# Sparse attention with a feed-forward block in split fp32: who issues the fetches of the weights, and where in a step they are converted

## The chip, the cores and the metric

The kernel runs on one core of a Trainium2 chip. The metric is the device time of one execution in microseconds (us). The engines are TensorE (PE, with its weight loads PEld), VectorE (DVE), ScalarE (ACT), GpSimd (POOL) and SyncE (SP); each works through its own instructions in the order in which they are written. SP computes nothing: before the change it issues most of the transfers.

## The reference

```python
# attention, per batch and head: B, H, S, D = 4, 8, 768, 64, blocks of 32
scores = scale * (q @ k^T)              # masked to: own block and its two neighbours, block 0 and the last,
                                        # 3 sampled blocks per block; rows of block 0 and the last see all
attn = exp(scores - max); attn /= sum + 1e-9
x = (attn @ v), as 3072 tokens x 512
# feed-forward: w_in 512 x 2048, w_out 2048 x 512, both float64
h = x @ w_in
out = (h * sigmoid(1.702 * h)) @ w_out  # float32
```

## The kernel before

**Steps of attention.** The 3072 tokens are 48 units of 64 tokens; a unit takes two steps (four for the units of the first and last blocks, which see all keys), 104 steps in all. A step t of the sparse kind does 16 small products of q and k (L252), takes the bias and the row's minimum on VectorE (L271, nm), exponentials on ScalarE (L284, ex), four transposes on PE (L299), their copy on ScalarE (L312, pt), and 32 products with V (L330). These are staggered: `tick` writes the scores of step t, the values of step t-2, then the transposes and the pt copy of step t-1. A finished unit is normalised (L347 to L350), turned (L360) and split into a high and a low fp32r part (L365 xhi, L366 xlo).

**Chunks of the feed-forward.** Eight units make a chunk of 512 tokens. For each of 6 chunks and each of 16 slices f of the hidden dimension there is one step m: `up` (12 matmuls, L447 to L449), `gate` (L455 on ScalarE, L456 on VectorE), its split (L461 ghi, L469 glo), and for the slice before, `down` (12 matmuls, L484 to L490). Beside each step m runs about one step of attention for the next chunk. The attention of the first chunk, 16 steps and two more, stands ahead of it all: the lead-in, with `early` true, in which score and transpose banks alternate. Then come the 16 steps of the first chunk's feed-forward, and so on.

**The weights.** They come as float64 and are turned into two fp32r parts, high and low. `weights` is a generator: each `next` writes one piece of work, up to a `yield`. It works through 32 conversions k, alternating slices of w_in and w_out: `todo` is (0, in), (1, in), (0, out), (2, in), (1, out) and so on. Conversion k has five pieces:

- ScalarE takes the absolute value of the high words of conversion k+1 (`first(k + 1)`, L393, a<-raw); VectorE limits it for k (L413)
- VectorE masks and shifts (L415)
- VectorE makes the low part of conversion k-1 (`last(k - 1)`, L398); for w_out both parts are then stored to a scratch tensor ws (L400); conversion k+2's words are fetched (`fetch(k + 2)`, L386, raw, 512 KB, one of three buffers)
- VectorE puts in the sign (L422)
- VectorE puts in the low words' bits (L425); ScalarE rounds to the high part (L428)

Before, the fetch and the store are on SP's queue. w_in's parts stay on the chip (`win`, 16 tiles); w_out's parts go through a ring of four tiles (`wout`), are stored, and come back from ws for the chunks after the first (L494). A w_out slice f is only converted when `down` of slice f-4 has been written, so a piece can do nothing for a while. `run` sets the pace: 3 pieces in a step of the lead-in, written between the scores and the transposes (`run(n0)`, ahead of `after`), and in the first chunk 4 ahead of the transposes and 4 at the end of each step m (`run(n1)`).

**K and V.** Each pair of batches has an entry per unit: K is 256 KB of q (L184) and 12 blocks of 128 KB (L186 to L196; the six sampled ones at addresses read from the table, L196), V is one direct part (vmid, L210 and L212) and two indirect gathers by POOL (vown, L214). Two buffers each: entry n+2 is loaded when entry n's last step is done, four steps ahead of its use. `loads` is called at the end of each step, and writes all K entries that are due, then all V entries. At the very start two of each are due: K0, K1, V0, V1. In the lead-in three of the six sampled K blocks are issued by POOL.

**Landing counters.** The transfers of SP and ScalarE share eight landing counters, taken in turn; a transfer is only issued when the one that last used its counter has landed.

Of the kernel before, what the change touches and what calls it, by code (L numbers as in the profile page):

```python
# [9 lines left out]
F32 = mybir.dt.float32  # L10
# [17 lines left out]
NF = DF // P  # L28
# [6 lines left out]
RING = 2  # L35
WRING = 4
# [7 lines left out]
class Kernel:  # L44
# [172 lines left out]

    def loads(self, t):

        while self.knext < len(self.kent) and (self.knext < RING or self.kent[self.knext - RING]["last"] <= t):  # L220
            self.load_k(self.kent[self.knext])
            self.knext += 1
        while self.vnext < len(self.vent) and (self.vnext < RING or self.vent[self.vnext - RING]["last"] <= t - 2):
            self.load_v(self.vent[self.vnext])
            self.vnext += 1

# [141 lines left out]
    def weights(self):  # L370

        nc = self.nc
        todo = []
        for f in range(NF + LAG):
            if f < NF:
                todo.append((f, 0))
            if f >= LAG:
                todo.append((f - LAG, 1))
        self.ready = set()
        tiles = {}  # L380

        def fetch(k):
            if k < len(todo):
                f, i = todo[k]
                raw = self.work.tile([P, 2 * DM], I32, name="raw", bufs=3)
                nc.sync.dma_start(out=raw, in_=self.w64[i][f])  # L386
                tiles[k] = {"raw": raw.rearrange("p (a b) -> p a b", b=2)}

        def first(k):

            if k < len(todo):
                a = tiles[k]["a"] = self.work.tile([P, DM], I32, name="a", bufs=3)
                nc.scalar.activation(out=a.bitcast(F32), in_=tiles[k]["raw"][:, :, 1].bitcast(F32), func=AF.Abs)  # L393

        def last(k):
            f, i = todo[k]
            t, w = tiles[k]["t"], tiles.pop(k)["a"].bitcast(F32)
            nc.vector.tensor_tensor(out=t[:, DM:2 * DM], in0=w, in1=t[:, 0:DM].bitcast(F32), op=ALU.subtract)  # L398
            if i == 1:
                nc.sync.dma_start(out=self.ws[f], in_=t.bitcast(F32))  # L400
            self.ready.add((f, i))

        for k in range(3):
            fetch(k)
        yield
        first(0)
        for k, (f, i) in enumerate(todo):
            while i == 1 and f - WRING > self.downs - 1:
                yield
            first(k + 1)  # L410
            raw, a = tiles[k]["raw"], tiles[k]["a"]
            low, high = raw[:, :, 0], raw[:, :, 1]
            nc.vector.tensor_scalar(out=a.bitcast(F32), in0=a.bitcast(F32), scalar1=FMIN, scalar2=None, op0=ALU.max)  # L413
            yield
            nc.vector.tensor_scalar(out=a, in0=a, scalar1=0x07FFFFFF, scalar2=3, op0=ALU.bitwise_and,  # L415
                                    op1=ALU.logical_shift_left)
            yield
            if k > 0:
                last(k - 1)
                fetch(k + 2)  # L420
                yield
            nc.vector.scalar_tensor_tensor(out=a, in0=high, scalar=-0x40000000, in1=a, op0=ALU.bitwise_and,  # L422
                                           op1=ALU.bitwise_or)
            yield
            nc.vector.scalar_tensor_tensor(out=a, in0=low, scalar=29, in1=a, op0=ALU.logical_shift_right,  # L425
                                           op1=ALU.bitwise_or)
            t = tiles[k]["t"] = self.win[f] if i == 0 else self.wout[f % WRING]
            nc.scalar.copy(out=t[:, 0:DM], in_=a.bitcast(F32))  # L428
            yield
        last(len(todo) - 1)  # L430

    def need(self, f, i):
        while (f, i) not in self.ready:
            next(self.conv, None)
# [88 lines left out]
    def tick(self, ts, m, n0, n1):  # L523
# [6 lines left out]
        for k in range(max(1, len(ts))):  # L530
            t = ts[k] if ts else None
            late = k == max(1, len(ts)) - 1
            un = None
            if t is not None:
                if have(t):
                    self.scores(t)
                if have(t - 2):
                    self.values(t - 2)
                    if self.steps[t - 2]["end"]:
                        un = self.steps[t - 2]["unit"]  # L540
            if late and moe:
                self.up(m)
            if un is not None:
                self.normalise(un)
            run(n0)
            after = []
            if t is not None:
                if have(t - 1):
                    after += self.transposes(t - 1)
                if un is not None:  # L550
                    after += self.turn(un)
            if late and moe:
                self.gate(m)
            for f in after:
                f()
            if t is not None:
                self.loads(t)
        if m is not None:
            if m >= LAG:
                self.down(m - LAG)  # L560
            if moe:
                self.gate_hi(m)
        run(n1)

    def run(self):
        self.g, self.downs = {}, 0
        self.conv = self.weights()
        self.indices()
        self.loads(-1)
        t = 0  # L570
        while t < self.ends[0] + LEAD:
            if t == 2:
                next(self.conv)
            self.tick([t], None, 3 if t > 3 else 0, 0)
            t += 1
        self.early = False
        total = len(self.steps) + 2
        for m in range(NC * NF + LAG):
            c, f = divmod(m, NF)
            if c + 1 < NC:  # L580
                goal = self.ends[c] + LEAD + (self.ends[c + 1] - self.ends[c]) * (f + 1) // NF
            else:
                goal = total
            ts = list(range(t, min(goal, total)))
            t = max(t, min(goal, total))
            self.tick(ts, m, 4 if c == 0 else 0, 4 if c == 0 else 0)

# [49 lines left out]
```

## Time and profile before

| | |
|---|---|
| median of 3 runs | 865.1 us (864.77 to 866.31) |
| the profiled execution | 869.51 us, its span 867.9 us |
| granted TensorE clock, mean | 0.965 |
| busy: PE, PEld, DVE, ACT, POOL | 783.5, 576.8, 374.3, 339.8, 57.5 us |
| moved by DMA | 153.38 MB, mean 177 GB/s |

The page shows the span in 40 slices of 21.7 us, each digit a busy share in tenths. A wait is put down to whatever ended it: "PE bank L330 <- ACT pt L312: 23.5, 9, 8.6" is 23.5 us in which PE, ahead of an instruction of line 330, waited for ScalarE's pt, in 9 pieces, the longest 8.6 us. SPq is SP's queue of issues. In rows of the timeline the two numbers ahead are start and duration in us, and the bracket behind is idle time and what ended it. Steps can be counted in the timeline by the first products of each step (L252) in the lead-in, and by the gates (L455) in the chunks.

### The profile page before, as it was taken

The page shows a single profiled execution, that of the slowest core. Times are in us where ns is not written, and L with a number is a line of the kernel's source. Part 1 is how long each engine was busy: PE and PEld are TensorE (multiplying, and loading weights), DVE is VectorE, ACT ScalarE, POOL GpSimd, SP SyncE. Part 2 cuts the span into 40 slices and gives each one's busy share as a digit, 9 for nine tenths or more (in the row PEclk, how much of TensorE's full clock was granted, in tenths as well). Part 3 has the DMA queues.
Part 4 walks back from the last instruction along what each step waited for, and adds up shares of the span by engine and source line. Part 5 has one row for each costly group of instructions (what it writes and reads, how often), then busy time and mean ns, then how long its engine had stood idle before and what let it go on. Part 6 is the DMA issues. An engine that isn't in the chain of part 4 may idle for free.

```text
span 867.9 us, 19160 instructions
## 1 busy us (share of the span) xinstructions
PE 783.5 (90%) x7584; PEld 576.8 (66%) x7584; DVE 374.3 (43%) x1026; ACT 339.8 (39%) x853; POOL 57.5 (7%) x85
## 2 busy tenths in 40 slices
PE   2547788788799999999999999999999999999996
PEld 0324556566576766767777777777776666778885
DVE  2466767667653333334333343333343343332222
ACT  2445544455443334334433344333443433322221
POOL 4121100100000000010000000000000000000000
PEclk9986889998999999999999999999999999999999
DMA  8887766666666444486655547454657432233221
GB/s 238 291 252 247 249 199 205 213 203 184 216 205 209 174 158 137 140 266 176 214 160 167 182 150 237 146 180 147 205 160 249 164 112 87 85 117 102 97 98 49
DMA packets 64285, 153.38 MB, mean 177 GB/s; under 512 B 7922, under 2 KB 29683, under 8 KB 63683
## 3 DMA queue, kind: packets, MB, share of 16 engines
q1 hardware_dynamic: 56962, 126.64, 46.0%
q0 software_dynamic: 7232, 25.51, 9.2%
q8 instruction: 60, 0.98, 0.5%
q14 instruction: 31, 0.25, 0.1%
HBM read 137.44 MB, written 14.68 MB: 175 GB/s over the span
## 4 chain that ended last, share of the span: by engine, by line
PE 74%; DMA 9%; DVE 5%; SPq 4%; ACT 3%; issue 3%; POOL 1%; POOLq 0%; ACTq 0%; DVEq 0%
PE bank L447 11%; PE bank L484 9%; PE bank L485 9%; PE bank L449 9%; PE bank L448 9%; PE bank L490 8%; DMA raw<-in_moe_w_in_dram 5%; PE bank L330 5%; PE bank L252 5%; PE bank L299 4%; PE bank L263 3%; DMA raw<-in_moe_w_out_dram 2%; DMA vown<-in_v_dram,vidx 1%; PE bank L337 1%; DVE bank L271 1%
## 5 line engine op out<-in xcount | busy, mean ns | idle before, releaser
L456 DVE SCALAR_TENSOR_TENSOR g<-g,bank 128x512 f32<-128x512 f32 x96 | 66.1, 688 | 282.1 <-ACT g L455 282.1
L447 PE MATMUL bank<-xhi,win 128*128 128x512 f32 x384 | 162.5, 423 | 0.0
L484 PE MATMUL bank<-wout,ghi 128*128 128x512 f32 x384 | 159.1, 414 | 0.0
L448 PE MATMUL bank<-xlo,win 128*128 128x512 f32 x384 | 152.4, 397 | 0.0
L449 PE MATMUL bank<-xhi,win 128*128 128x512 f32 x384 | 152.4, 397 | 0.0
L485 PE MATMUL bank<-wout,ghi 128*128 128x512 f32 x384 | 152.0, 396 | 0.0
L284 ACT ACTIVATE ex<-bank,nm 128x256 f32<-128x256 f32 x176 | 81.7, 470 | 164.5 <-DVE nm L271 163.3
L455 ACT ACTIVATE g<-bank 128x512 f32<-128x512 f32 x96 | 57.3, 597 | 177.5 <-PE bank L449 177.4
L271 DVE CUSTOM_DVE_ANT_1 bank<-bank,bias 128x256 f32<-128x256 f32 x176 | 71.5, 448 | 84.1 <-PE bank L252 76.2
L490 PE MATMUL bank<-wout,glo 128*128 128x512 f32 x360 | 98.6, 395 | 0.0
L252 PE MATMUL bank<-kg,qt 64*32 64x256 f32 x1408 | 65.9, 422 | 30.6 <-ACT pt L312 17.7
L447 PEld LDWEIGHTS bank<-xhi,win 128*128 128x128 f32 x384 | 73.7, 192 | 20.6 <-issue 0.5
L449 PEld LDWEIGHTS bank<-xhi,win 128*128 128x128 f32 x384 | 73.6, 192 | 17.0
L448 PEld LDWEIGHTS bank<-xlo,win 128*128 128x128 f32 x384 | 74.2, 193 | 13.1
L330 PEld LDWEIGHTS bank<-vown,pt 128*32 128x32 f32 x1408 | 32.5, 116 | 75.1 <-issue 33.7
L469 DVE TENSOR_TENSOR glo<-g,ghi 128x512 fp32r<-128x512 f32 x96 | 66.4, 691 | 36.7 <-ACT ghi L461 36.3
L485 PEld LDWEIGHTS bank<-wout,ghi 128*128 128x128 f32 x384 | 73.0, 190 | 13.4
L484 PEld LDWEIGHTS bank<-wout,ghi 128*128 128x128 f32 x384 | 72.7, 189 | 13.6
L214 POOL DMA_INDIRECT vown<-in_v_dram,vidx x44 | 44.3, 1007 | 563.9 <-PE bank L330 446.6
L330 PE MATMUL bank<-vown,pt 128*32 128x64 f32 x1408 | 52.0, 237 | 32.8 <-ACT pt L312 24.4
L490 PEld LDWEIGHTS bank<-wout,glo 128*128 128x128 f32 x360 | 68.1, 189 | 16.2
L312 ACT COPY pt<-bank 128x512 f32<-128x512 f32 (+1 forms) x120 | 65.2, 556 | 14.7 <-PE bank L299 11.2
(69 smaller groups left out, 753.2 us busy)
## 6 DMA issues: line engine op xcount, KB each, us to landing
wout<-ws SPq DMA_DIRECT2D x80, 512.0 KB, 3.4
kg<-in_kb_dram SPq DMA_DIRECT2D x158, 128.0 KB, 3.1
raw<-in_moe_w_in_dram SPq DMA_DIRECT2D x16, 512.0 KB, 5.6
raw<-in_moe_w_out_dram SPq DMA_DIRECT2D x16, 512.0 KB, 5.7
ws<-wout SPq DMA_DIRECT2D x16, 512.0 KB, 4.1
kg<-in_kb_dram SPq DMA_DIRECT2D x26, 256.0 KB, 4.1
kg<-in_kT_dram SPq DMA_DIRECT2D x4, 1536.0 KB, 7.8
vown<-in_vd_dram SPq DMA_DIRECT2D x8, 768.0 KB, 5.5
```

What stands on the lines that cost most here:

```text
L252: nc.tensor.matmul(sps[h][BLK * c:BLK * (c + 1), 0:n].rearrange("p (g n s) -> p g n s", g=2, n=4), self.qt[r][rows, bi, UT * pair + BLK * ...
L271: nc.vector.tensor_tensor_reduce(out=at, in0=at, in1=bias, scale=-SCALE, scalar=3.0e38, op0=ALU.add, op1=ALU.min, accum_out=nm[:, c:c + 1])
L284: nc.scalar.activation(out=ex, in_=sms[c], func=AF.Exp, bias=least[c], scale=-1.0, accum_out=sums[c])
L330: nc.tensor.matmul(av[BLK * c:BLK * (c + 1), 2 * i + h], pt[:, 2 * h + k, BLK * c:BLK * (c + 1)], src[:, at:at + D], start=(k == 0), stop= ...
L447: nc.tensor.matmul(h, wih[:, k], hi[:, k], start=(k == 0), stop=False)
L448: nc.tensor.matmul(h, wih[:, k], lo[:, k], start=False, stop=False)
L449: nc.tensor.matmul(h, wil[:, k], hi[:, k], start=False, stop=(k == NCT - 1))
L456: nc.vector.scalar_tensor_tensor(out=g, in0=g, scalar=1.0, in1=self.h, op0=ALU.add, op1=ALU.mult)
L469: self.nc.vector.tensor_tensor(out=glo, in0=g, in1=ghi.bitcast(F32), op=ALU.subtract)
L484: nc.tensor.matmul(o[n], ghi[:, tk[n]], woh, start=(f == 0), stop=False)
L485: nc.tensor.matmul(o[n], ghi[:, tk[n]], wol, start=False, stop=False)
L490: nc.tensor.matmul(o[n], glo[:, tk[n]], woh, start=False, stop=False)
```

## The change

Four things change. The fetches of words (`fetch`) are issued by ScalarE instead of SP. The stores of w_out's parts are issued by ScalarE too, and written later: conversion k's store stands in conversion k+2, behind its fetch, as a function `save` of its own. `loads` takes K and V entries in turn, so the start has K0, V0, K1, V1. And in the lead-in the three pieces of conversion stand at the end of a step, behind the transposes, the pt copy and `loads`, instead of ahead of the transposes. What is left of the conversion after the 16 steps of the first chunk is written out ahead of the next step.

```diff
     def loads(self, t):
-        while self.knext < len(self.kent) and (self.knext < RING or self.kent[self.knext - RING]["last"] <= t):
-            self.load_k(self.kent[self.knext])
-            self.knext += 1
-        while self.vnext < len(self.vent) and (self.vnext < RING or self.vent[self.vnext - RING]["last"] <= t - 2):
-            self.load_v(self.vent[self.vnext])
-            self.vnext += 1
+        more = True
+        while more:
+            more = False
+            if self.knext < len(self.kent) and (self.knext < RING or self.kent[self.knext - RING]["last"] <= t):
+                self.load_k(self.kent[self.knext])
+                self.knext += 1
+                more = True
+            if self.vnext < len(self.vent) and (self.vnext < RING or self.vent[self.vnext - RING]["last"] <= t - 2):
+                self.load_v(self.vent[self.vnext])
+                self.vnext += 1
+                more = True
...
-                nc.sync.dma_start(out=raw, in_=self.w64[i][f])
+                nc.scalar.dma_start(out=raw, in_=self.w64[i][f])
...
             nc.vector.tensor_tensor(out=t[:, DM:2 * DM], in0=w, in1=t[:, 0:DM].bitcast(F32), op=ALU.subtract)
+            self.ready.add((f, i))
+
+        def save(k):
+            f, i = todo[k]
             if i == 1:
-                nc.sync.dma_start(out=self.ws[f], in_=t.bitcast(F32))
-            self.ready.add((f, i))
+                nc.scalar.dma_start(out=self.ws[f], in_=self.wout[f % WRING].bitcast(F32))
...
                 last(k - 1)
                 fetch(k + 2)
                 yield
+            if k > 1:
+                save(k - 2)
...
+        save(len(todo) - 2)
         last(len(todo) - 1)
+        yield
+        save(len(todo) - 1)
...
-            self.tick([t], None, 3 if t > 3 else 0, 0)
+            self.tick([t], None, 0, 3 if t > 3 else 0)
...
+            if m == NF:
+                for _ in self.conv:
+                    pass
```

The lines behind the edits move down, by 5 at L284 (now L289) and by 13 at L455 (now L468). POOL's queue at the start, before: kg_93 is K0's buffer, kg_94 K1's, vown_97 and vown_98 V0's and V1's (each sampled block is read from the table, then issued).

```order
L196 DMA kg_93<-in_kb_dram 128x256
L195 TENSOR_LOAD sbr
L195 ISA x2
L196 ISA
L196 DMA kg_94<-in_kb_dram 128x256
...
L196 DMA kg_94<-in_kb_dram 128x256
L214 DMA vown_97<-in_v_dram,vidx 128x1024 x2
L214 DMA vown_98<-in_v_dram,vidx 128x1024 x2
```

And after:

```order
L196 DMA kg_93<-in_kb_dram 128x256
L214 DMA vown_97<-in_v_dram,vidx 128x1024 x2
L195 TENSOR_LOAD sbr
L195 ISA x2
L196 ISA
L196 DMA kg_94<-in_kb_dram 128x256
...
L196 DMA kg_94<-in_kb_dram 128x256
L214 DMA vown_98<-in_v_dram,vidx 128x1024 x2
```

V0's two gathers now stand behind K0's last block, ahead of K1's three. ScalarE in the lead-in, before, two steps (ex is L284, pt L312):

```order
L284 ACTIVATE ex,rs<-bank_85,nm 128x256
L284 ACTIVATE ex,rs<-bank_86,nm 128x256
L393 ACTIVATE a<-raw 128x512
L312 COPY pt<-bank_92 128x512
L284 ACTIVATE ex,rs<-bank_89,nm 128x256
L284 ACTIVATE ex,rs<-bank_90,nm 128x256
L428 CAST win_104<-a 128x512
L393 ACTIVATE a<-raw 128x512
L312 COPY pt<-bank_88 128x512
```

And after, the same place (ex is L289, pt L317, a<-raw L398, the cast L438):

```order
L289 ACTIVATE ex,rs<-bank_85,nm 128x256
L289 ACTIVATE ex,rs<-bank_86,nm 128x256
L317 COPY pt<-bank_92 128x512
L398 ACTIVATE a<-raw 128x512
L391 DMA raw<-in_moe_w_in_dram 128x1024
L289 ACTIVATE ex,rs<-bank_89,nm 128x256
L289 ACTIVATE ex,rs<-bank_90,nm 128x256
L317 COPY pt<-bank_88 128x512
L370 CAST xhi_121<-bank_91 128x4x64
L438 CAST win_104<-a 128x512
L398 ACTIVATE a<-raw 128x512
```

The conversion's rows stand behind pt instead of ahead of it, and the fetch stands in this queue, one step ahead of the row that uses its words. ScalarE in the first chunk, before (g is the gate, ghi its high part):

```order
L393 ACTIVATE a<-raw 128x512
L284 ACTIVATE ex,rs<-bank_85,nm 128x256
L284 ACTIVATE ex,rs<-bank_86,nm 128x256
L428 CAST wout_117<-a 128x512
L393 ACTIVATE a<-raw 128x512
L455 ACTIVATE g<-bank_92 128x512
L312 COPY pt<-bank_85 128x512
L461 CAST ghi<-g 128x512
L428 CAST win_107<-a 128x512
```

And after:

```order
L398 ACTIVATE a<-raw 128x512
L391 DMA raw<-in_moe_w_out_dram 128x1024
L409 DMA ws_72<-wout_120 128x1024
L289 ACTIVATE ex,rs<-bank_85,nm 128x256
L289 ACTIVATE ex,rs<-bank_86,nm 128x256
L438 CAST wout_117<-a 128x512
L398 ACTIVATE a<-raw 128x512
L391 DMA raw<-in_moe_w_in_dram 128x1024
L468 ACTIVATE g<-bank_92 128x512
L317 COPY pt<-bank_85 128x512
L474 CAST ghi<-g 128x512
L438 CAST win_107<-a 128x512
```

Each fetch now stands behind the use of the words fetched before it, and a store stands right behind a fetch; the rest keeps its order.

## Prediction

> **What bounds the kernel now.** I began with the page's slices, to see which part of the span has time to win.
>
> ```profile
> PE   2547788788799999999999999999999999999996
> DMA  8887766666666444486655547454657432233221
> ```
>
> TensorE (PE) is saturated from about slice 12 (250 us) to the end; what can move lies before. There I took a table by stage (busy time of PE, PEld, DVE, ACT, POOL, then granted clock, DMA share, GB/s): the start, the rest of the lead-in (attention of the first chunk), the first chunk's feed-forward with the conversion of the weights, and a stretch behind it.
>
> ```profile
> 0.00:29.00 29.00, 7.58 (x88) 3.50 (x88) 6.12 (x34) 4.72 (x14) 10.28 (x33) 1.00 0.89 259
> 29.00:93.00 64.00, 39.36 (x805) 23.64 (x812) 41.12 (x133) 34.61 (x99) 15.13 (x20) 0.80 0.81 259
> 93.00:250.00 157.00, 133.66 (x1280) 97.37 (x1280) 105.37 (x252) 74.61 (x173) 9.64 (x9) 0.91 0.66 210
> 250.00:310.00 60.00, 57.32 (x653) 42.43 (x652) 23.69 (x72) 25.17 (x67) 1.87 (x2) 1.00 0.59 191
> ```
>
> PE is idle for 21, 25 and 23 us in the first three stages, and no engine is full there. So waits decide. Who waits in the lead-in (total, times, longest):
>
> ```profile
> PE bank L330 <- ACT pt L312: 23.5, 9, 8.6
> ACT a L393 <- DMA raw<-in_moe_w_in_dram: 7.3, 2, 6.3
> ```
>
> and in the first chunk:
>
> ```profile
> ACT a L393 <- DMA raw<-in_moe_w_in_dram: 24.2, 9, 5.2
> PE bank L252 <- ACT pt L312: 15.1, 8, 4.1
> ACT a L393 <- DMA raw<-in_moe_w_out_dram: 15.7, 4, 6.2
> PE bank L299 <- ACT ex L284: 7.3, 4, 4.0
> SPq L400 <- DVE wout L398: 72.8, 9, 11.3
> ```
>
> This is one chain: SP's queue stands still at a store (L400) until VectorE has made the second half of a weight, a fetch (L386) behind it goes out late, ScalarE stands at L393 until the words land, and PE stands at what ScalarE has queued behind (pt, ex). One place shows it, SP, ScalarE and PE in turn:
>
> ```profile
> 143.67 6.05 SPq L196 DMA_DIRECT2D kg<-in_kb_dram  x6
> 149.82 0.38 SPq L386 DMA_DIRECT2D raw<-in_moe_w_out_dram  x1
> 153.82 0.66 ACT L393 ACTIVATE a<-raw 128x512 f32<-128x512 f32 x1 [3.98 <-DMA raw<-in_moe_w_out_dram]
> 154.98 0.66 PE L299 MATMUL bank<-ident,ex 128*128 128x128 f32 x4 [4.01 <-ACT ex L284]
> ```
>
> Here it is six K loads that hold the fetch up, and the 4 us end on PE. The fetch itself took 4.0 us (149.82 to 153.82); over all, the median landings are
>
> ```profile
> raw<-in_moe_w_in_dram SPq DMA_DIRECT2D x16, 512.0 KB, 5.6
> raw<-in_moe_w_out_dram SPq DMA_DIRECT2D x16, 512.0 KB, 5.7
> ```
>
> **The change part by part.** The profiled execution took 869.5 us (span 867.9, 1.6 around it), 4.4 us over the median of 865.1; I sum differences on the profile and take them off the median.
>
> *K and V in turn.* Rows of POOL, ScalarE and PE at the start:
>
> ```profile
> 9.72 0.54 POOL L196 DMA_DIRECT2D kg<-in_kb_dram  x1 [0.64 <-issue]
> 13.21 1.01 POOL L214 DMA_INDIRECT vown<-in_v_dram,vidx  x1 [0.58 <-issue]
> 17.45 0.58 ACT L312 COPY pt<-bank 128x512 f32<-128x512 f32 x1
> 26.95 0.43 PE L330 MATMUL bank<-vown,pt 128*32 128x64 f32 x5 [2.75 <-DMA vown<-in_v_dram,vidx]
> ```
>
> PE could start its first values when pt is copied (18.0) and starts them in full at 26.95, when V has landed. The change puts V's two gathers ahead of the second K's three loads on POOL, at 9.72 instead of 13.21: 3.5 us at least. If V then lands before pt, 8.9 us. The second K must then land later, but is first needed two steps on. I take 5, nearer the lower end, since the DMA share there is 0.89 and the landing is mostly a backlog. **-5** (-8.9 to -3.5).
>
> *Lead-in: conversion behind the step, fetches on ScalarE.* From the first row to the second it runs 15 steps in 63.9 us; the other four rows serve the next part.
>
> ```profile
> 29.00 1.11 PE L252 MATMUL bank<-kg,qt 64*32 64x256 f32 x16
> 92.88 1.11 PE L252 MATMUL bank<-kg,qt 64*32 64x256 f32 x16
> 99.91 0.60 ACT L455 ACTIVATE g<-bank 128x512 f32<-128x512 f32 x1 [1.03 <-PE bank L449]
> 242.72 0.60 ACT L455 ACTIVATE g<-bank 128x512 f32<-128x512 f32 x1 [0.31 <-PE bank L449]
> 250.31 0.60 ACT L455 ACTIVATE g<-bank 128x512 f32<-128x512 f32 x1 [1.95 <-PE bank L449]
> 265.23 0.60 ACT L455 ACTIVATE g<-bank 128x512 f32<-128x512 f32 x1 [1.93 <-PE bank L449]
> ```
>
> Without its waits for words a step is (63.9 - 7.3)/15 = 3.8 us. pt now goes ahead of the conversion, so a late word no longer holds values; next late is the following step's ex, which PE needs a step later. On ScalarE a fetch stands one step ahead of its use, so each of 7 fetches waits for its landing less 3.8. Landing 4.0 (the row at 149.82): 1.4 us in all, against 7.3: -6. Landing 5.7: 13.3, +6. Transfers bound the gain: 259 GB/s over 64 us is 16.6 MB, which at the best slice's 291 GB/s takes 57 us:
>
> ```profile
> GB/s 238 291 252 247 249 199 205 213 203 184 216 205 209 174 158 137 140 266 176 214 160 167 182 150 237 146 180 147 205 160 249 164 112 87 85 117 102 97 98 49
> ```
>
> I take a landing of 4.7, above the one below, as the DMA share is 0.81 here and 0.66 there (6.3 us of waits, -1), and 2 us for the cover that the new place gives: **-3** (-7 to +6).
>
> *First chunk.* 15 steps in 142.8 us (99.91 to 242.72), 9.52 each; undisturbed they take 7.45 (250.31 to 265.23 is two). So 31 us can be won at most. What a conversion costs, by line:
>
> ```profile
> L393 ACT ACTIVATE a<-raw 128x512 f32<-128x512 f32 x32 | 21.2, 666 | 47.3 <-DMA raw<-in_moe_w_in_dram 31.4 <-DMA raw<-in_moe_w_out_dram 15.7
> L428 ACT CAST win<-a 128x512 fp32r<-128x512 f32 x16 | 9.9, 619 | 18.7 <-DVE a L425 18.7
> L425 DVE SCALAR_TENSOR_TENSOR a<-raw,a 128x512 int32<-128x512 int32 x32 | 22.1, 690 | 0.8
> L422 DVE SCALAR_TENSOR_TENSOR a<-raw,a 128x512 int32<-128x512 int32 x32 | 22.0, 686 | 0.0
> L398 DVE TENSOR_TENSOR wout<-a,wout 128x512 fp32r<-128x512 f32 x16 | 11.0, 687 | 1.2 <-ACT wout L428 1.2
> L415 DVE TENSOR_SCALAR a<-a 128x512 int32<-128x512 int32 x32 | 13.7, 429 | 0.9
> L413 DVE TENSOR_SCALAR a<-a 128x512 f32<-128x512 f32 x32 | 13.5, 421 | 4.9 <-ACT a L393 4.9
> ```
>
> A conversion has 5 pieces and a step runs 8, so 1.6 conversions per step, one per 4.65 us. A fetch stands 3 pieces ahead of the use of its words: 2.8 us. Two things change in opposite senses. Gone is all that held a fetch in SP's queue: the stores' 72.8 us and the K loads. But on ScalarE fetch k+2 stands behind L393 of k+1, which waits for its own words: one fetch is under way at a time, where SP often had two. So every one of 24 conversions waits for landing less 2.8. With a landing of 4.5, between 4.0 and 5.7 and nearer the lower since store and K loads are no longer ahead in the same queue, that is 1.7 x 24 = 41 us, as much as today's 24.2 + 15.7. What differs is the size of a piece: ScalarE's idle time takes up small ones. Its own work per step is 25.17/60 x 7.45 = 3.1, plus 1.6 x (0.67 + 0.62) = 2.1, plus 2.4 issues (1.6 fetches, 0.8 stores) at the 0.38 of SP's row = 0.9: 6.1 of 7.45, idle 0.8 per conversion. So (1.7 - 0.8) x 24 = 22 us remain of 31: -9, and I take **-8**, for ScalarE also waits for L425. Landing 4.0 gives 0.4 x 24 = 10, -21; landing 5.7 gives 2.1 x 24 = 50, +19. It breaks even at 4.9. VectorE sets a floor: 23.69/60 x 7.45 + 1.6 x 2.91 = 7.6 us per step, so at most -29.
>
> *Waits and work added.* The 48 issues are counted above; in the lead-in ScalarE works 34.6 of 64 us, and 11 of them (4 us) lie in its idle time, up to +4 if not. Each transfer also waits for the landing of an earlier one (eight landing counters go round); on SP this costs
>
> ```profile
> SPq L386 <- DMA kg<-in_kb_dram: 1.6, 2, 0.8
> ```
>
> and nobody minds; on ScalarE it would hold ex and pt, and so PE. +2 (0 to 5). Finishing the conversion ahead of step 16 puts one or two VectorE operations ahead of its scores: +1 (0 to 2). SP's K and V loads lose their wait behind the stores, which is worth nothing after the start: their buffers come free four steps ahead.
>
> Sum: -5 - 3 - 8 + 2 + 1 = -13, kept in full, since PE is saturated behind: **852 us**.
>
> The Trainium skill, "DMA: Bandwidth & Descriptors", section "Issuing engines are not separate DMA queues", says that transfers from all issuers share the same 16 engines, so that a second issuer saves only sequencer time. By it the landing would stay near 5.7 and the sum would be that of the first rival. The rows speak half against it: here the sequencer time saved is large, as SP's queue stands at a wait.
>
> **The rivals.**
> *Slower: one fetch in flight.* ScalarE waits for each landing in turn. It decides from a landing of 4.9. At 5.7: -5 + 6 + 19 + 3 = +23, 888 us; at 5.1 (lead-in 7 x 1.3 - 7.3 - 2 = 0, first chunk 1.5 x 24 - 31 = +5), -5 + 0 + 5 + 3 = +3, 868 us. For it: the DMA share of 0.81 in the lead-in, and medians of 5.6 and 5.7; against it: these include the queue that goes. 0.28.
> *Only the start counts.* Smaller waits in more places cancel, landing about 4.9: -5 + 3 = -2, 863 us (860 to 867). 0.18.
> *Landings near 4.0*, VectorE the next bound: -6 - 6 - 21 + 1 = -32, 833 us. For it: the row at 149.82; against it: K loads still run beside. 0.12.
>
> **How the numbers follow.** My forecast, 0.42, has 843 to 859 as its own range (landings of 4.3 to 4.8 throughout, by the same formulas). A run can tell 0.2%, 1.7 us, from no change. Faster: 0.42 + 0.12 + 0.08 of the second rival = 0.62; same 0.07; slower 0.28 + 0.03 = 0.31. The range from 838 to 878 leaves out half of the third rival and the far end of the first.
>
> **What would show it.** Right: the first full group at L330 before 23 us; PE's wait for pt in the lead-in under 12 us; median landing of raw under 4.9; gates of the first chunk under 9.2 us apart; ScalarE's waits for raw more in number, none over 4 us. Wrong: landings over 5, gates 10 us apart, or a wait of ScalarE's queue for K's landings of more than 5 us in all.

## The result, and the profile after

The change took the kernel from 865.7 us (median of 4 runs) to 844.5 us (842.25 to 847.82, 4 runs): a ratio of 0.9748, 95% interval 0.970 to 0.9796. That is faster by 21 us; 852 was forecast, with 838 to 878 as the range. The profiled execution took 845.2 us, its span 843.5, 24.4 us less than the span of before.

The slices first: PE is now full from slice 11.

```profile
PE   3656898989999999999999999999999999999996
DMA  8888777767675426577554656545465523142232
```

The same table by stage, with its borders at the places of before (the scores of step 3, step 18, and the gate of step m = 16, which was at 250.3 and is at 227.6):

```profile
0.00:21.70 21.70, 7.55 (x90) 3.50 (x90) 6.10 (x34) 3.81 (x11) 10.51 (x33) 1.00 0.87 273
21.70:84.80 63.10, 38.69 (x805) 22.23 (x808) 39.93 (x130) 35.92 (x104) 13.80 (x19) 0.80 0.87 279
84.80:227.60 142.80, 130.03 (x1284) 95.63 (x1284) 106.03 (x254) 74.87 (x174) 9.58 (x9) 0.94 0.73 231
227.60:287.60 60.00, 57.32 (x653) 42.48 (x652) 24.03 (x72) 25.50 (x68) 1.88 (x2) 1.00 0.61 200
```

Two borders lie elsewhere on the clock, so read the work, not the lengths: busy times are nearly those of before, and what has gone is mostly idle time, PE's in the third stage above all (12.8 us now, 23.3 before). PE's busy time in that stage is 3.6 us less too, for the same matmuls, at a granted clock of 0.94 instead of 0.91. From the gate at 227.6 to the end it is 615.9 us, against 617.6 before: the rest of the kernel has not moved, and whatever was won ahead of it is kept.

Two more marks of the lead-in and three of the first chunk, on PE and ScalarE:

```profile
19.64 0.43 PE L335 MATMUL bank<-vown,pt 128*32 128x64 f32 x5 [0.81 <-DMA vown<-in_v_dram,vidx]
30.57 1.42 PE L257 MATMUL bank<-kg,qt 64*32 64x256 f32 x16 [5.47 <-DMA vmid<-in_v_dram]
84.75 0.68 PE L257 MATMUL bank<-kg,qt 64*32 64x256 f32 x8
92.73 0.58 ACT L468 ACTIVATE g<-bank 128x512 f32<-128x512 f32 x1
221.97 0.60 ACT L468 ACTIVATE g<-bank 128x512 f32<-128x512 f32 x1 [1.13 <-DVE wout L403]
227.55 0.60 ACT L468 ACTIVATE g<-bank 128x512 f32<-128x512 f32 x1 [1.43 <-PE bank L462]
```

The first values start in full at 19.6 us instead of 26.95. But step 4's scores stand at a landing until 30.57, where before they began at 32.62:

```profile
32.62 0.64 PE L252 MATMUL bank<-kg,qt 64*32 64x256 f32 x8
```

Step 18 comes at 84.8 (before 92.9), the first gate at 92.7 (99.9), the sixteenth at 222.0 (242.7), the next at 227.6 (250.3). So 7 us are won by the first gate, 13.6 in the first chunk's 15 steps (129.2 us, before 142.8), 2 more in the step behind.

The waits of the lead-in and of the first chunk answer to those shown of before (their line numbers have moved):

```profile
PE bank L335 <- ACT pt L317: 14.7, 9, 3.4
ACT a L398 <- DMA raw<-in_moe_w_out_dram: 3.4, 3, 1.6
```

```profile
ACT a L398 <- DMA raw<-in_moe_w_out_dram: 17.0, 9, 3.7
PE bank L257 <- ACT pt L317: 7.8, 5, 3.3
ACT a L398 <- DMA raw<-in_moe_w_in_dram: 5.3, 5, 2.1
PE bank L304 <- ACT ex L289: 4.9, 4, 2.5
```

ScalarE's waits for words in the first chunk are 22.3 us in 14 pieces, where they were 39.9 in 13; PE's behind them 12.7 instead of 22.4. SP's wait at the store is no more in the list. The landings:

```profile
raw<-in_moe_w_in_dram ACTq DMA_DIRECT2D x16, 512.0 KB, 4.4
raw<-in_moe_w_out_dram ACTq DMA_DIRECT2D x16, 512.0 KB, 5.6
```

### The profile page after: what moved, and what is told of

It reads as the page before. It is cut to its first block, busy times and chain, and to the rows that moved or that the text cites. A ratio compares the mean times of both kernels' runs of the same rounds, so it can differ in the third digit from the quotient of the medians.

```text
span 843.5 us, 19136 instructions
## 1 busy us (share of the span) xinstructions
PE 777.3 (92%) x7584; PEld 572.0 (68%) x7584; DVE 373.6 (44%) x1026; ACT 340.5 (40%) x853; POOL 56.4 (7%) x85
## 4 chain that ended last, share of the span: by engine, by line
PE 76%; DMA 12%; DVE 5%; ACT 3%; issue 1%; SPq 1%; ACTq 0%; DVEq 0%
PE bank L460 11%; PE bank L497 10%; PE bank L498 10%; PE bank L462 9%; PE bank L461 9%; PE bank L503 9%; DMA raw<-in_moe_w_out_dram 7%; PE bank L257 4%; PE bank L335 4%; PE bank L304 3%; DMA raw<-in_moe_w_in_dram 3%; PE bank L268 3%; DMA kg<-in_kb_dram 1%; PE bank L342 1%; PE bank L312 1%
## 5 line engine op out<-in xcount | busy, mean ns | idle before, releaser
L461 PE MATMUL bank<-xlo,win 128*128 128x512 f32 x384 | 150.7, 393 | 0.0
L289 ACT ACTIVATE ex<-bank,nm 128x256 f32<-128x256 f32 x176 | 81.8, 470 | 168.6 <-DVE nm L276 165.0
L468 ACT ACTIVATE g<-bank 128x512 f32<-128x512 f32 x96 | 57.4, 598 | 178.4 <-PE bank L462 174.6
L460 PEld LDWEIGHTS bank<-xhi,win 128*128 128x128 f32 x384 | 72.7, 189 | 19.9 <-issue 0.3
L462 PEld LDWEIGHTS bank<-xhi,win 128*128 128x128 f32 x384 | 72.6, 189 | 16.7
L498 PEld LDWEIGHTS bank<-wout,ghi 128*128 128x128 f32 x384 | 73.3, 191 | 13.6
L474 ACT CAST ghi<-g 128x512 fp32r<-128x512 f32 x96 | 59.7, 622 | 20.3 <-DVE g L469 20.3
L317 ACT COPY pt<-bank 128x512 f32<-128x512 f32 (+1 forms) x120 | 65.4, 557 | 6.0 <-PE bank L312 3.0
## 6 DMA issues: line engine op xcount, KB each, us to landing
kg<-in_kb_dram SPq DMA_DIRECT2D x158, 128.0 KB, 3.3
```

Of the source, the lines that this page charges most:

```text
L289: nc.scalar.activation(out=ex, in_=sms[c], func=AF.Exp, bias=least[c], scale=-1.0, accum_out=sums[c])
L460: nc.tensor.matmul(h, wih[:, k], hi[:, k], start=(k == 0), stop=False)
L461: nc.tensor.matmul(h, wih[:, k], lo[:, k], start=False, stop=False)
L462: nc.tensor.matmul(h, wil[:, k], hi[:, k], start=False, stop=(k == NCT - 1))
L498: nc.tensor.matmul(o[n], ghi[:, tk[n]], wol, start=False, stop=False)
```

## The experiments

The theory: in SP's queue a store that waits for VectorE stands ahead of a fetch, and whatever parts the two wins. Rivals: the start is what counts; the place of the conversion is; or one fetch in flight on ScalarE costs as much as the queue did. Each ratio is to the kernel before, timed on the same chip (its medians there were 865.7 to 868.0). The marks in this table are read from each profiled execution; waits are ScalarE's waits for words (us, pieces) from the first gate on. The rows shown further down count from step 18, a little earlier.

| kernel | median us | ratio (95%) | step 18 | gates 0, 15, 16 | waits, pieces |
|---|---|---|---|---|---|
| before | 865.7 | 1 | 92.9 | 99.9, 242.7, 250.3 | 37.7, 12 |
| the change | 844.5 | 0.9748 (0.970 to 0.9796) | 84.8 | 92.7, 222.0, 227.6 | 22.3, 14 |
| a1, K and V in turn alone | 861.3 | 0.9944 (0.9921 to 0.9966) | 87.2 | 95.1, 236.3, 243.3 | 36.6, 11 |
| a2, conversion behind the step alone | 858.2 | 0.991 (0.9876 to 0.9945) | 85.1 | 92.3, 233.1, 240.7 | 36.6, 11 |
| a3, fetches on ScalarE alone | 847.6 | 0.9772 (0.9737 to 0.9807) | 86.9 | 95.9, 223.9, 230.6 | 29.0, 15 |
| a4, stores on ScalarE and late alone | 847.2 | 0.9774 (0.9742 to 0.9806) | 85.7 | 91.1, 224.6, 230.5 | 21.6, 6 |
| a5, stores late on SP alone | 851.2 | 0.9823 (0.979 to 0.9855) | 87.7 | 94.7, 228.5, 235.6 | 23.3, 6 |
| b1, the change without turns | 851.1 | 0.9815 (0.9779 to 0.9852) | 89.3 | 97.0, 225.6, 231.9 | 23.2, 16 |
| b2, the change, fetches on SP | 843.3 | 0.9725 (0.9696 to 0.9754) | 81.2 | 88.4, 219.0, 226.1 | 19.3, 7 |
| b4, the change, first fetches later | 844.6 | 0.9752 (0.9725 to 0.9779) | 81.3 | 88.3, 218.2, 224.5 | 22.7, 14 |
| b3, the change, early fetches | 827.0 | 0.9548 (0.952 to 0.9576) | 80.1 | 85.7, 203.5, 209.1 | 3.2, 4 |
| c4, b3 with fetches on SP | 828.2 | 0.956 (0.9525 to 0.9595) | 77.4 | 82.9, 205.9, 211.5 | 14.8, 5 |
| d1, before, early fetches alone | 833.5 | 0.9622 (0.9591 to 0.9653) | 83.6 | 90.8, 208.6, 215.4 | 11.8, 6 |
| c1, b3 and b4 | 823.1 | 0.9502 (0.947 to 0.9534) | 76.9 | 82.4, 197.1, 202.7 | 2.0, 3 |

A second table takes the stretch from step 18 to gate 16, in which PE does the same matmuls in every kernel, from one profiled execution of each (us; waits are ScalarE's waits for words there):

| kernel | length | PE busy | PE idle | granted clock | waits, pieces |
|---|---|---|---|---|---|
| before | 157.4 | 134.1 | 23.3 | 0.91 | 39.9, 13 |
| the change | 142.8 | 130.0 | 12.8 | 0.94 | 22.3, 14 |
| a3 | 143.7 | 126.2 | 17.5 | 0.98 | 31.8, 16 |
| a4 | 144.8 | 130.4 | 14.4 | 0.93 | 21.6, 6 |
| b2 | 144.9 | 130.4 | 14.5 | 0.93 | 20.6, 8 |
| c4 | 134.1 | 125.0 | 9.1 | 0.99 | 14.8, 5 |
| d1 | 131.8 | 124.3 | 7.5 | 0.99 | 11.8, 6 |
| b3 | 129.0 | 124.2 | 4.8 | 0.99 | 3.8, 5 |

Two things shorten it. In all but b3, where little is left, PE is idle 0.55 to 0.7 us for each us that ScalarE waits, in small pieces as in large ones. And PE's busy time falls with a rising granted clock. The clock is highest where PE idles least, a3 apart; whether the idling lowers it is not shown.

**One part alone: K and V in turn (a1).** The new `loads`, nothing else:

```diff
-        while self.knext < len(self.kent) and (...):
+        more = True
+        while more:
...
```

> Only K and V loads in turn, all else as before. Theory A (the start counts): the first values begin some 7 us earlier and the gain stays, 858 us. Theory B (the start is bound by what all transfers of the first 30 us move): the wait goes from V0 to K1 at step 4, and of the 7 us 2 or fewer are left, 863 to 866 us.

861.3 us, 0.56% less than before. The first values come at 19.5 us instead of 26.95, and step 4 indeed waits, but only until 26.2:

```profile
26.19 0.67 PE L257 MATMUL bank<-kg,qt 64*32 64x256 f32 x10 [1.10 <-DMA vmid<-in_v_dram]
```

Step 18 comes 5.7 us earlier, and some 5 us are kept at the end. The result lies between the two theories: 858 was too low, and more than 2 us are left.

**One part alone: the conversion behind the step (a2).**

```diff
-            self.tick([t], None, 3 if t > 3 else 0, 0)
+            self.tick([t], None, 0, 3 if t > 3 else 0)
```

> Only the conversion at the end of a step in the lead-in; fetches and stores stay on SP. Theory A (place): PE's wait for pt, 23.5 us in the lead-in, falls to half and step 18 comes 6 us earlier, 859 us. Theory B (the queue counts): the words still land late behind SP's stores, ScalarE stands as long in another place, and less than 3 us are won, 862 to 867 us.

858.2 us, 0.9% less. Step 18 comes at 85.1, 7.8 us earlier, and PE's wait for pt between steps 3 and 18 is

```profile
PE bank L330 <- ACT pt L312: 9.9, 9, 1.8
```

instead of 23.5. Theory A: in the lead-in the new place helps even with the queues as they were. It is not the only cure there: a3 and a4, with the conversion at its old place, bring step 18 to 86.9 and 85.7. In the first chunk little changes (140.8 us for 15 steps, before 142.8).

**One part alone: fetches on ScalarE (a3).**

```diff
-                nc.sync.dma_start(out=raw, in_=self.w64[i][f])
+                nc.scalar.dma_start(out=raw, in_=self.w64[i][f])
```

> Only the fetches of words issued by ScalarE; stores stay on SP at their old place. Theory A (a fetch behind the stores and K loads in SP's queue is what costs): most of the change is here, 849 to 853 us, ScalarE's waits for words in the first chunk fall from 39.9 us to under 28. Theory B (one fetch in flight costs as much as the queue did): 860 to 868 us with as much waiting as before.

847.6 us: nearly all that the whole change wins. ScalarE's waits for words in the first chunk are

```profile
ACT a L393 <- DMA raw<-in_moe_w_out_dram: 19.4, 10, 3.0
ACT a L393 <- DMA raw<-in_moe_w_in_dram: 12.4, 6, 3.4
```

31.8 us, not under 28: in sum much nearer to the 39.9 of before than the gain is. The time is Theory A's, the waits are between the two. The 15 steps take 128.0 us, 14.8 less, with 16 pieces of at most 3.4 us in place of 13 of up to 6.2. That small pieces cost PE less does not follow. In the stretch of the second table ScalarE waits 8.1 us less and PE idles 5.8 us less, about as much per us as before; the other 7.9 us are PE's busy time, at a granted clock of 0.98 instead of 0.91:

```profile
86.94:230.60 143.66, 126.17 (x1284) 92.75 (x1284) 105.68 (x253) 74.51 (x174) 9.73 (x10) 0.98 0.71 230
```

No run separates this clock from the edit.

**One part alone: the stores (a4, a5).** a4 is the kernel before with the change's `save`, two conversions late, and the rest of the conversion ahead of step 16:

```diff
-            if i == 1:
-                nc.sync.dma_start(out=self.ws[f], in_=t.bitcast(F32))
...
+        def save(k):
+            f, i = todo[k]
+            if i == 1:
+                nc.scalar.dma_start(out=self.ws[f], in_=self.wout[f % WRING].bitcast(F32))
...
+            if k > 1:
+                save(k - 2)
```

a5 is a4 with `save` on SP:

```diff
-                nc.scalar.dma_start(out=self.ws[f], in_=self.wout[f % WRING].bitcast(F32))
+                nc.sync.dma_start(out=self.ws[f], in_=self.wout[f % WRING].bitcast(F32))
```

> Only the stores issued by ScalarE and two conversions later (with the rest of the conversion written out ahead of step 16); fetches stay on SP. Theory A (SP's queue stands at stores, and the fetch behind them is late): the 88.6 us of SP's waits at the store go and half the gain of the first chunk comes with them, 855 to 859 us. Theory B (K loads hold the fetches up as much): 861 to 866 us.

> Only the stores two conversions later (with the rest of the conversion written out ahead of step 16), still issued by SP; fetches on SP as before. Theory A (a store costs because SP's queue stands at it until VectorE has made the low part; two conversions later that part is long made): as much as with the stores on ScalarE, 846 to 849 us. Theory B (the store has to leave SP's queue, since its 512 KB go ahead of the fetch in it): 854 to 862 us.

a4: 847.2 us, as much as the fetches alone; both theories expected less of it. The waits of its first chunk:

```profile
ACT a L393 <- DMA raw<-in_moe_w_out_dram: 14.3, 4, 4.7
ACT a L393 <- DMA raw<-in_moe_w_in_dram: 7.3, 2, 4.9
```

w_in's words, the ones fetched behind a store, are awaited twice instead of nine times; those of w_out, fetched behind K loads, four times as before. SP's queue does not stand much less, it stands elsewhere: no longer at the store, but at the fetch itself, until VectorE has done with the buffer (L430 is here what L425 was before):

```profile
SPq L386 <- DVE a L430: 82.1, 20, 10.8
```

So the fetch goes out as soon as its buffer is free: over the conversions from k = 11 on, a median of 0.07 us after, where before it was 3.0. In a5 the stores never leave SP, and 1.8% of a4's 2.3% is there, a time between its two theories: most of it is that no fetch stands behind a store that waits for VectorE. The rest, about 0.5%, has intervals that overlap, and I leave open whether it is the 512 KB ahead of the fetch in one queue.

Alone, the four parts win 0.56, 0.9, 2.28 and 2.26%, 6.0% in sum; together 2.5%. a3 and a4 cure the same thing, so one of them is enough: b2 tests that from the other side.

**The change without turns (b1), and with the fetches back on SP (b2).** b1 is the change with the `loads` of before, a1's diff the other way round. b2 is the change and

```diff
-                nc.scalar.dma_start(out=raw, in_=self.w64[i][f])
+                nc.sync.dma_start(out=raw, in_=self.w64[i][f])
```

> The change without K and V in turn. Theory A (the 5 us that this part wins alone add to the rest): 5 us slower than the change, 849 us. Theory B (the start only moves a wait, since transfers bound the whole lead-in): within 2 us of the change, 843 to 847 us, step 18 of the lead-in within 2 us of the change's 84.8.

> The change with the fetches back on SP, the stores left on ScalarE at their late place. Theory A (what costs is a fetch behind a store that waits for VectorE in one queue; either edit cures it): within 3 us of the change, 842 to 848 us. Theory B (SP's K loads hold the fetches up too, and ScalarE's issue is needed for that): 850 to 856 us.

b1: 851.1 us (844.75 to 853.53), step 18 at 89.3 instead of 84.8. By the medians Theory A: the turns win some 6 us also beside the rest, although step 4 is only 1 us earlier for them (30.6 against 31.6); where the others come from is not shown. Its runs scatter and its interval overlaps the change's, so the size is uncertain; the profile has 4.3 us at gate 16 (231.9 against 227.6). b2: 843.3 us, 0.9725 against the change's 0.9748, the same. Theory A: with the stores gone from SP, who issues the fetches makes no difference to the time. It does to its parts. From SP the fetches go out a median of 0.07 us after their buffers are free, from ScalarE 3.3 us after, where they are written; but on SP a few stand behind K loads, and ScalarE then waits up to 4.3 us for one. Step 18 comes 3.6 us earlier than with the change, and the stretch behind it is 2.1 us longer.

**Early fetches (b3).** The change, and

```diff
                 last(k - 1)
-                fetch(k + 2)
                 yield
...
             nc.scalar.copy(out=t[:, 0:DM], in_=a.bitcast(F32))
+            fetch(k + 3)
             yield
```

The buffer of conversion k is free when its last VectorE operation is done, which the cast ahead of the new place waits for anyway. Two fetches can then be in flight.

> The change with each fetch three pieces earlier, at the end of the conversion that frees its buffer, so that two are in flight on ScalarE's queue and a fetch stands five pieces ahead of its use. Theory A (one fetch in flight, waiting for its landing, is what is left in the first chunk): ScalarE's waits for words fall from 22 us to under 5, gates come 8.0 us apart instead of 8.6, 834 to 838 us. Theory B (VectorE, or ScalarE's own work, sets the first chunk): the waits fall but the time stays within 3 us, 841 to 846 us.

827.0 us, 4.5% less than before and better than Theory A had it. The same waits in the first chunk:

```profile
ACT a L398 <- DMA raw<-in_moe_w_in_dram: 2.6, 3, 1.7
ACT a L398 <- DMA raw<-in_moe_w_out_dram: 1.2, 2, 0.7
PE bank L257 <- ACT pt L317: 4.2, 5, 2.1
PE bank L304 <- ACT ex L289: 0.5, 2, 0.2
```

The landings on record are few, 2 of 16 for w_in (8.6 us at the start, 4.0 later) and 3 of 16 for w_out. They leave open whether landings got shorter: behind the start they took 3.6 to 4.3 us, but the four fetches from k = 11 on that ScalarE still waited for were a median of 5.6 us old. The medians:

```profile
raw<-in_moe_w_in_dram ACTq DMA_DIRECT2D x16, 512.0 KB, 6.3
raw<-in_moe_w_out_dram ACTq DMA_DIRECT2D x16, 512.0 KB, 3.6
```

What differs for certain is the distance: over the conversions from k = 11 on, 6.4 us lie between a fetch and the use of its words, of which ScalarE waits 0.15; with the change 5.1 and 0.95. So late fetches are what the change still paid for, 18.5 us at gate 16. Of these 4.7 are there at step 18; behind it PE idles 8.0 us less and is busy 5.8 us less, at a clock of 0.99 instead of 0.94. The mean distance alone does not give the time: in b2 it is 6.5 us too, but 0.84 are waited, for b2's few late fetches, and before the change it was 6.5 with 1.8 waited, the fetches behind a store late and others early. What b3 brings is that hardly any is late: 1.0 us behind its free buffer at most. The gates from m = 1 to 15 are now 7.9 us apart:

```profile
92.65 0.60 ACT L468 ACTIVATE g<-bank 128x512 f32<-128x512 f32 x1 [1.65 <-issue]
203.53 0.60 ACT L468 ACTIVATE g<-bank 128x512 f32<-128x512 f32 x1 [1.13 <-DVE wout L403]
```

Between these two rows PE is busy 108.2 of 110.9 us and VectorE 94.1, so it is PE that is full, not VectorE:

```profile
92.65:203.53 110.88, 108.16 (x1091) 79.75 (x1090) 94.09 (x223) 64.66 (x149) 8.18 (x8) 1.00 0.74 247
```

**Early fetches without ScalarE (c4), and without the rest of the change (d1).** c4 is b3 with b2's diff; d1 is the kernel before with b3's.

> The change with early fetches, issued by SP instead of ScalarE (stores stay on ScalarE). Theory A (distance to the use decides, the issuer does not): 824 to 830 us, as with early fetches on ScalarE. Theory B (K loads ahead in SP's queue make some fetches late again): 832 to 840 us, ScalarE's waits for words over 10 us.

> The kernel before with only the fetches three pieces earlier, on SP; stores at their old place on SP. Theory A (a fetch is late only because it stands behind the store that VectorE ends last; now it stands ahead of that store): most of the change's gain without ScalarE, 843 to 850 us. Theory B (the K loads and the older store in the same queue still hold it): 853 to 862 us.

c4: 828.2 us, as b3: the time is Theory A's, though ScalarE waits 14.8 us in 5 pieces, as B had it. As in b2, two differences cancel: step 18 comes 2.7 us earlier than in b3, and the stretch behind it takes 5.1 us longer. Against b2, where the same queue has the fetch three pieces later, c4 wins 15 us: 3.8 at step 18 and 10.8 behind it, half of these idle time and half busy time at the higher clock. d1: 833.5 us, 3.8% less than before: two lines, without ScalarE, without late stores or turns, win half as much again as the whole change. Its waits:

```profile
ACT a L393 <- DMA raw<-in_moe_w_in_dram: 9.1, 4, 4.0
ACT a L393 <- DMA raw<-in_moe_w_out_dram: 2.7, 2, 1.8
```

SP's queue still holds a few fetches up, and there is time enough for most.

**The first fetches one step later (b4), and both (c1).**

```diff
-            if t == 2:
+            if t == 3:
                 next(self.conv)
```

> The change with the first three fetches one step later (ahead of step 3 instead of step 2). Theory A (they take K1's bandwidth, so step 4 waits until 30.6): step 4 begins at 26 to 28 us, and 2 to 3 us are won, 841 us. Theory B (transfers bound the lead-in as a whole, so bytes put off are late elsewhere): step 4 comes earlier, step 18 does not, 843 to 847 us.

> The change with early fetches on ScalarE and the first three fetches one step later. Theory A (step 4 no longer waits for K1 beside three fetches): 3 us less than with early fetches alone, 822 to 825 us. Theory B (transfers bound the lead-in): 825 to 829 us, the same.

b4: 844.6 us, 0.9752, not to be told from the change, although in its profile step 4 starts at 26.2 instead of 30.6 and gate 16 at 224.5 instead of 227.6: inconclusive. With early fetches the medians differ: c1 takes 823.1 us, 0.9502, Theory A's time and the lowest here. Step 4 starts at

```profile
25.08 0.67 PE L257 MATMUL bank<-kg,qt 64*32 64x256 f32 x10 [1.47 <-issue]
```

Against b3, timed in another set, the intervals just overlap, so the gain is likely and not shown; the profiles differ by 3.2 us at step 18 and 6.4 at gate 16.

## Why the prediction was right, point by point

**K and V in turn: -5.** Right in size: 4.8 us alone (0.56% of 865.7), 4.3 at gate 16 when taken out of the change. My account was incomplete. V does land 7.3 us earlier, within the bounds, but in the change step 4 then waits for the second K (the profile names V's vmid, but the scores read K and q alone), and I wrote that it "is first needed two steps on" as if that made it free. So of the 7.3 us 2.1 are left at step 4, and how they come to be 4 or 5 later is open.

**The lead-in: -3.** Too small. Alone the new place wins 7.8 us at step 18; in the change, from step 4 to 18, it is 54.2 us where it was 60.3. The reason given holds: a late word no longer holds pt, and PE's wait for pt fell from 23.5 to 14.7 us, short of the "under 12" that I asked for, and to 9.9 in a2. The term was mis-sized because I let landings set it and allowed the place 2 us. Nor is the place the only cure: a3 and a4, without it, bring step 18 6.0 and 7.2 us earlier. The bound from 291 GB/s was no bound: b3's lead-in moved 303 at a DMA share of 0.93.

```profile
21.40:80.10 58.70, 38.58 (x801) 23.02 (x800) 39.98 (x130) 35.48 (x104) 13.63 (x19) 0.91 0.93 303
```

**The first chunk: -8.** Measured -13.6, with another 2 us in the step behind. The term was mis-sized, because two steps of it failed.

The first is "every one of 24 conversions waits for landing less 2.8", 41 us, as much as before: ScalarE's waits for words fell from 39.9 to 22.3 us. From k = 11 on, 5.1 us lie between fetch and use and 0.95 of them are waited, so the cover is 4.1: three pieces of five took longer than three fifths of an undisturbed conversion. That ScalarE's other waits, for VectorE and for PE, fall between them is likely the reason; I did not measure it. Hence the break-even landing of 4.9 was also wrong. In a3, where ScalarE waited for a landing, the fetch was a median of 5.7 us old, for which the formula gives +19, and the chunk still gained 14.8 us.

The second is "What differs is the size of a piece: ScalarE's idle time takes up small ones". PE was idle 0.58 us for each us of waiting before, at 3.1 us a piece, and 0.57 with the change, at 1.6: the size of a piece made no difference that shows. In the stretch of the second table PE idles 10.5 us less because there is less waiting, and it is busy 4.1 us less at the higher granted clock, a term that the prediction does not have.

**Waits and work added: +3.** Half found. ScalarE does now wait for K's landings, with ex behind, once for 3.5 us:

```profile
ACT ex L289 <- DMA kg<-in_kb_dram: 3.5, 1, 3.5
```

The +1 for finishing the conversion ahead of step 16 was not there; that step took 5.6 us instead of 7.6.

**The rivals.** The mechanism of the first, one fetch in flight, is there: b3 removes it, together with the lateness of each fetch, and 17 us go. But b2 does not have it either and gains nothing, so the number in flight alone is not the cost. And it cost less than the queue it replaced, at landings (4.4 and 5.6) which I had called the break-even region; the second was a sign that I had named of being wrong. The Trainium skill's rule, "DMA: Bandwidth & Descriptors", section "Issuing engines are not separate DMA queues", that a second issuer saves only sequencer time, agrees with b2 and c4, where the issuer made no difference (0.9725 against 0.9748, 0.956 against 0.9548). It does not tell what that time is worth: in a3 it was 2.3%, because SP's sequencer stood at a wait. The third rival's time, 833, is passed by b3; whether with landings near 4.0 its few records do not tell, but its next bound, VectorE, is not what b3 meets: there PE is full.

The sum came out at -13 for -21 because every term but the start was read from landings, where what counts is whether a fetch goes out late for its use. That 852 came near is in part luck. With a landing of 5.0, the mean of the two medians of the change (5 and 3 landings of 16 are on record), the prediction's own formulas give -5 - 1 + 3 + 3 = 0, no gain: a landing taken too short made up for a cover taken too short. What was right is the chain itself, a fetch behind a store that waits for VectorE, which a3, a4 and a5 cut one at a time.

## What to carry to other kernels

In a queue that works in order, ask of each transfer what stands ahead of it and what that waits for: a store that waits for the last engine of a chain should not stand ahead of a load that starts the next one. Moving either cures it, and doing both wins it once. A queue with little else to do, as SP's here, issues most transfers as soon as their waits end, even if they are written later; on an engine that computes, the place in the program sets the time. Early writing pays on both, since it also takes a fetch ahead of other loads in its queue (c4 against b2, 15 us). Before changing the issuer, see how early the buffer comes free: the fetch written at that point, two lines on the kernel before, won 3.8%, the whole change 2.5%.

## What the runs showed of the hardware

Where a transfer is written and when it goes out can be far apart. Written at the same place, a fetch went out a median of 0.07 us after its buffer was free on SP (a4, b2) and 3.3 us after on ScalarE (the change); written three pieces earlier, on ScalarE, 0.09 us after (b3).

Fewer waits came with faster matmuls. From step 18 to gate 16 the same matmuls kept PE busy for 134.1 us before, at a granted clock of 0.91, and for 124.2 us in b3, at 0.99, while its idle time fell from 23.3 to 4.8 us. Clock and idle time go together in most of these runs, not in a3; that one causes the other was not tested.

And a load that starts later can help the ones ahead of it: three fetches of 512 KB begun a step later brought step 4's scores from 30.6 to 26.2 us in b4. Where SP issues these three behind K's loads, step 4 starts at 26.2 (a1), 25.4 (b2) and 25.3 us (c4). This fits K's last blocks having to share the transfers' rate with the fetches; I did not measure the share itself, and b4's total time does not show the gain.
